# Attention with 64 heads on one core: Q and K rows interleaved by dimension, V and ones in alternate columns, seven output buffers, other planner numbers and a rewritten end

## The chip, the core and the metric

The kernel runs as one program on 1 core of a Trainium2 chip. Its time is the device time of one execution in microseconds (us); a kernel's time is the median of its runs. TensorE is called PE below, VectorE DVE, ScalarE ACT, GpSimd POOL and SyncE SP, as the profile does.

## The reference

Two attentions over the same 2048 tokens, 32 heads of 16 dimensions each, are mixed by a gate. In A all heads share one K and one V, in B every head has its own.

```
def _A_ref(x, wq, wk, wv, wo):          # H = 32, Dh = 16, S = 2048, D = 512
    q = (x @ wq).reshape(B, S, H, Dh).transpose(0, 2, 1, 3)
    k = x @ wk
    v = x @ wv
    scores = jnp.einsum("bhqd,bkd->bhqk", q, k) * (Dh ** -0.5)
    p = _softmax(scores, axis=-1)
    o = jnp.einsum("bhqk,bkd->bhqd", p, v)
    return o.transpose(0, 2, 1, 3).reshape(B, S, H * Dh) @ wo
...
x = A_x
g = _sigmoid((x * gate_w).sum(-1, keepdims=True))
a = _A_ref(x, A_wq, A_wk, A_wv, A_wo)
b = _B_ref(x, B_wqkv, B_wo)             # as A, but q, k, v all per head, from one wqkv
return g * a + (1 - g) * b
```

## The kernel before

**Work and stages.** The 64 heads go in eight groups of eight, alternately from A and B (`groups`, n = 0 to 7). A group has two halves of the queries, and a half has two parts, q = 0 and q = 2, of two head pairs each. That makes 32 phases. In a phase 32 key blocks ("quads") are worked for two head pairs, so a phase has 64 score tiles, the kernel 2048. A score tile is [128 keys, 2 heads x 512 queries]: PE multiplies K with Q into PSUM (`products`), ACT takes exp of it into an SBUF tile called prob (`score`, line 622), and PE multiplies V with that (`values`, line 663). Two PSUM buffers named sc hold the scores. A stationary operand of V has 32 columns, 16 of V and 16 of ones, so numerator and denominator of the softmax come out of one product, summed in a third PSUM buffer over the phase.

**Exp on VectorE.** Some score tiles skip ACT. Their scores go to the other PSUM buffer of the two named `pair`, and DVE computes exp in seven instructions (`chain`): a conversion to int32 (line 816), two bit operations (819, 823) and four steps of a polynomial (828). The results lie in tiles named vec.

**Precision.** Q and K are split into a high and a low fp16 half. A head's 16 dimensions take 64 rows: Q has high, low, high, low and K has high, high, low, low, 16 rows each. `lay` (line 383) moves the halves from the projection to these rows by DMA, on the queues of SP and POOL.

**The end of a phase.** `emptied` has DVE copy the sums to an SBUF tile raw (line 722). `normalised` moves the denominators to a tile dT and the numerators to oT by ten DMAs on SP (line 546); DVE then takes reciprocals (553), multiplies (556), and splits into o16, high and low (559, 562). `o_unit` multiplies o16 with the output weights on PE, DVE scales by the gate into a tile named sum (line 506), and a DMA adds it to the output. In the last group (n = 7) the sum is made in SBUF instead, in `late`, which lies in the memory of xT (line 500).

**What sets the order.** The whole program is written out by a planner that runs when the kernel is built. `_Plan` carries estimated clocks of the engines; `pe_step` chooses what PE does next (a score tile, a piece of `values`, or a step of another unit); `plan.vector` chooses what DVE does next. `vector_job` decides when a score tile goes to DVE: not while more than WORK nanoseconds of chain work are queued, not without three free vec tiles, and from within the last MOST quads of a phase, or the next phase when fewer than CHAIN nanoseconds are left. A projection of Q may begin EARLY quads ahead of the half before the one that needs it. `hurry` gives other units precedence when their due time is near, with JOB, AFTER and SPARE as their prices. Engines run what they are given in order and wait on semaphores, so a wrong estimate shows as a wait, not as another order.

**The end of the kernel.** After the last exp (lines 1225 to 1237) the last raw is normalised in four pieces of 128 tokens; ACT makes the high half (559), POOL the low half (562), PE three products per piece into the same PSUM buffer, DVE two adds (500), and SP and ACT send two blocks out.

Of the kernel before, what the change touches and what calls it, by code (L numbers as in the profile page):

```python
# [49 lines left out]
ISSUE, ISSUE_SP, LANDS, SUM_LANDS = 480, 600, 3200, 6500  # L50
PROBS, VECS = 6, 7

# [112 lines left out]
def _fast(ctx, tc, x, wq_a, wk_a, wv_a, wo_a, wqkv_b, wo_b, gate_w, out, flag):  # L165
# [165 lines left out]
    def kv_split(h, bank):  # L331
# [3 lines left out]
        k32 = ops.tile([P, 2, 4, DH], F32, tag="k32", name=f"k32{h}", bufs=1)  # L335
        kn = sums[1][:, h].bitcast(F16).rearrange("p (i a b d) -> p i a b d", i=8, a=2, b=4)
        ts = slice(8 * h, 8 * h + 8)

        def take(queue=nc.sync, key=True, value=True):
            if key:  # L340
                nc.vector.tensor_scalar(k32, pk[:, :, :, :DH], UP ** -1, None, op0=ALU.mult)
            if value:
                for d in (0, 2 * DH):
                    v = vA[0][:, ts, d : d + DH].rearrange("p (e i) d -> p e i d", e=2)
                    nc.vector.tensor_scalar(v, pk[:, :, :, DH : 2 * DH], UP ** -2, None, op0=ALU.mult)
                swapped(vA[1][:, ts], vA[0][:, ts], queue)
                nc.vector.tensor_copy(z[:, ts].rearrange("p (e i) -> p e i", e=2), pk[:, :, :, 2 * DH])
# [13 lines left out]
    def k_turn(kn, bank, i):  # L361
        pkt = bank[:, 0].bitcast(F16)
        nc.tensor.transpose(pkt[:, i * P : (i + 1) * P], kn[:, i].rearrange("p a b d -> p (a b d)"), ident16)

# [18 lines left out]
    def lay(hilo, to, p, parts, queues):  # L383

        fns = []
        for n, part in sorted(enumerate(parts * 2), key=lambda x: x[1]):
            hh = n // 4
            at = slice((2 * p + hh) * DH, (2 * p + hh + 1) * DH)
            dst = to[hh * ROWS + n % 4 * DH :][:DH].rearrange("d (a q) -> d a q", a=2)
            fns.append(lambda q=queues[len(fns) % len(queues)], dst=dst, src=hilo[part][at]: q.dma_start(dst, src))  # L390
        return fns
# [89 lines left out]
    def o_unit(n, half, t, qs, first, last):  # L481
# [55 lines left out]
    def normalised(n, half, q, raw, now):  # L537
# [4 lines left out]
        queues = (nc.sync, nc.scalar, nc.gpsimd) if ends else (nc.sync,)  # L542
        moves = [(d, DH, 2 * DH, 0), (d, 5 * DH, 2 * DH, 2 * DH), (o, 0, DH, 0), (o, 3 * DH, 2 * DH, DH), (o, 7 * DH, DH, 3 * DH)]
        moves = [(*move, e) for part in (0, 2) for e in range(2) for move in moves[part : part + 2 + part // 2]]
        for m, (part, at, n_rows, to, e) in enumerate(moves):
            queues[m % len(queues)].dma_start(part[ROWS * e + to :][:n_rows], raw[at : at + n_rows, e])  # L546
# [14 lines left out]
        def low(c):  # L561
            (nc.gpsimd if ends else nc.vector).tensor_sub(o16[:, 1, c : c + cut], o[:, c : c + cut], o16[:, 0, c : c + cut])

# [86 lines left out]
    def values(m, cols):  # L650
# [5 lines left out]
        for k in range(4):  # L656
            p, hh = q + k // 2, k % 2
            if src == "a":
                v = vA[w][:, c, hh * DH : (hh + 2) * DH]
            else:  # L660
                v = vB[w][:, c, p, hh : hh + 2, :].rearrange("p a d -> p (a d)")
# [47 lines left out]
    def emptied(t):  # L709
# [10 lines left out]
        def take():  # L720
            state["raw"] = ops.tile([P, 2, BLK], F32, tag="raw", name=f"raw{ph}", bufs=1)
            nc.vector.tensor_copy(state["raw"], full)  # L722

# [285 lines left out]
    def flag_stats():  # L1009
        absmax("v_a", 0, vA[0][:, :, :DH], AX.XY)  # L1010
        absmax("gate", 0, wkv16[0][:, 0, :, 2 * DH])
# [123 lines left out]
    pair_q = (nc.sync, nc.gpsimd)  # L1135
    moves = [lay(hilo, to[p], p, (0, 1, 0, 1), (nc.scalar,) * 2 + pair_q * 3 if p == 1 else pair_q) for p in range(4)]
    for move in moves[0][:4] + moves[1][:4] + moves[0][4:] + moves[1][4:]:
        move()
# [85 lines left out]

    over, times, high, low = tail[0]
    last = [o_unit(len(groups) - 1, 1, t, (2,), False, True) for t in range(4)]
    over(0), times(0), high(0), low(0)
    for t in range(4):
        if t < 3:
            c = (t + 1) * P  # L1230
            over(c), times(c), high(c), low(c)
        for fn, _ in last[t].jobs:
            fn()
        last[t].finish(plan.pe)
        for op in plan.ops:
            op.fn()
        plan.ops.clear()

# [148 lines left out]
```

## Time and profile before

| | before |
|---|---|
| median of 3 runs | 1860.64 us (1858.08 to 1861.57) |
| the profiled execution: own time, span | 1863.72 us, 1861.9 us |
| busy: ACT, PE, DVE, POOL | 1797.5, 1760.7, 1217.5, 392.0 us |
| exp tiles on ACT in the trace | 1932 into prob, 12 into vec |
| exp tiles on DVE (line 816) | 104 |
| granted PE clock, mean | 0.992 |

The span is from the first instruction to the last; the profiled execution's own time holds 1.8 us more around it. Busy time is the union of an engine's instructions. A row of the groups gives the count, the busy time, the mean length of one instruction in ns and then the idle time of the engine ahead of it with what ended it. A row of the timeline gives start and length in us.

### The profile page before, as it was taken

The page shows a single profiled execution, that of the slowest core. Times are in us where ns is not written, and L with a number is a line of the kernel's source. Part 1 is how long each engine was busy: PE and PEld are TensorE (multiplying, and loading weights), DVE is VectorE, ACT ScalarE, POOL GpSimd, SP SyncE. Part 2 cuts the span into 40 slices and gives each one's busy share as a digit, 9 for nine tenths or more (in the row PEclk, how much of TensorE's full clock was granted, in tenths as well). Part 3 has the DMA queues.
Part 4 walks back from the last instruction along what each step waited for, and adds up shares of the span by engine and source line. Part 5 has one row for each costly group of instructions (what it writes and reads, how often), then busy time and mean ns, then how long its engine had stood idle before and what let it go on. Part 6 is the DMA issues. An engine that isn't in the chain of part 4 may idle for free.

```text
span 1861.9 us, 97691 instructions
## 1 busy us (share of the span) xinstructions
PE 1760.7 (95%) x45403; PEld 859.8 (46%) x45403; DVE 1217.5 (65%) x1369; ACT 1797.5 (97%) x1959; POOL 392.0 (21%) x575
## 2 busy tenths in 40 slices
PE   9999999999999999999999999999999999998994
PEld 5544454444444444444444445444444444443441
DVE  4267323969686772678677684297868677349963
ACT  4999999999999999999999999999999999999993
POOL 4213103232031211412112320242202320130000
PEclk9999999999999999999999999999999999999997
DMA  5121212223142322412224240252313322234011
GB/s 146 41 60 43 82 32 55 82 57 57 32 79 40 66 49 59 83 35 54 43 50 75 51 80 21 51 97 48 57 40 54 65 53 45 51 66 124 24 49 59
DMA packets 75678, 109.69 MB, mean 59 GB/s; under 512 B 22256, under 2 KB 30672, under 8 KB 75264
## 3 DMA queue, kind: packets, MB, share of 16 engines
q0 software_dynamic: 27904, 44.24, 14.1%
q1 hardware_dynamic: 43920, 56.51, 11.9%
q8 instruction: 357, 5.85, 1.4%
q10 hardware_dynamic: 3440, 2.62, 0.4%
q14 instruction: 57, 0.47, 0.1%
HBM read 14.82 MB, written 33.55 MB: 26 GB/s over the span
## 4 chain that ended last, share of the span: by engine, by line
ACT 74%; PE 11%; issue 8%; DVE 5%; DMA 1%; SPq 1%; POOL 0%; ACTq 0%; DVEq 0%
ACT prob L622 74%; PE pair L663 5%; PE sc L608 3%; DVE vec L828 2%; PE pair L207 2%; DVE vec L816 1%; SPq L546 1%; DVE xT L500 0%; DVE dT L553 0%; DVE sum L506 0%; PE pt L294 0%; PE pair L294 0%; PE pair L457 0%; DVE vec L819 0%; DVE raw L722 0%
## 5 line engine op out<-in xcount | busy, mean ns | idle before, releaser
L622 ACT ACTIVATE prob<-sc 128x1024 f32<-128x1024 f32 x1932 | 1777.0, 1125 | 12.3 <-PE sc L608 10.4
L663 PE MATMUL pair<-prob,vA 64*32 64x512 f32 (+1 forms) x8168 | 521.8, 566 | 0.8 <-issue 0.8
L663 PE MATMUL pair<-prob,vB 64*32 64x512 f32 (+1 forms) x8112 | 521.7, 570 | 0.5 <-issue 0.5
L608 PE MATMUL sc<-Qb,K 64*32 64x512 f16 x7744 | 409.5, 381 | 47.0 <-ACT prob L622 38.7
L608 PE MATMUL sc<-Qa,kA 64*32 64x512 f16 x7808 | 409.5, 381 | 20.4 <-ACT prob L622 12.3
L608 PEld LDWEIGHTS <-K 64*32 64x32 f16 x8192 | 203.8, 90 | 422.9 <-issue 382.9
L608 PEld LDWEIGHTS <-kA 64*32 64x32 f16 x8192 | 202.9, 90 | 390.3 <-issue 349.9
L828 DVE SCALAR_TENSOR_TENSOR vec<-vec,vec 128x1024 f32<-128x1024 f32 x312 | 378.3, 1224 | 2.6
L663 PEld LDWEIGHTS pair<-prob,vA 64*32 64x32 f32 x8168 | 158.7, 105 | 23.7 <-issue 4.8
L663 PEld LDWEIGHTS pair<-prob,vB 64*32 64x32 f32 x8112 | 157.8, 105 | 22.2 <-issue 2.7
L816 DVE TENSOR_SCALAR vec<-pair 128x1024 int32<-128x1024 f32 x104 | 126.4, 1215 | 51.6 <-PE pair L608 49.3
L828 DVE SCALAR_TENSOR_TENSOR vec<-vec 128x1024 f32<-128x1024 f32 x104 | 131.3, 1263 | 1.2
L516 POOL DMA_DIRECT2D out_dram<-sum x48 | 60.1, 1253 | 340.7 <-DVE sum L506 330.8
L553 DVE RECIPROCAL dT<-dT 128x256 f32<-128x256 f32 (+1 forms) x66 | 111.4, 1693 | 28.2 <-DMA dT<-raw 28.2
L722 DVE COPY raw<-pair 128x1024 f32<-128x1024 f32 x32 | 39.2, 1224 | 115.3 <-PE pair L663 115.2
L506 DVE TENSOR_SCALAR sum<-pair,gate_up 128x512 f32<-128x512 f32 x112 | 79.2, 742 | 49.2 <-PE pair L207 49.1
L390 POOL DMA_DIRECT2D K<-hikb x64 | 31.1, 491 | 341.7 <-DVE hikb L431 340.9
L390 POOL DMA_DIRECT2D Qa<-hiqa x63 | 31.9, 511 | 335.7 <-DVE hiqa L431 316.9
L207 PE MATMUL pair<-w16ob,o 64*32 64x512 f16 x1536 | 66.1, 392 | 14.8 <-ACT o L559 6.9
L823 DVE TENSOR_SCALAR vec<-vec 128x1024 int32<-128x1024 int32 x104 | 78.1, 751 | 0.0
L819 DVE TENSOR_SCALAR vec<-vec 128x1024 int32<-128x1024 int32 x104 | 75.2, 723 | 1.4
L431 DVE TENSOR_SCALAR hivb<-pair 128x1024 f16<-128x1024 f32 x8 | 9.8, 1224 | 101.2 <-PE pair L207 101.2
(149 smaller groups left out, 1272.2 us busy)
## 6 DMA issues: line engine op xcount, KB each, us to landing
out_dram<-sum POOLq DMA_DIRECT2D x48, 512.0 KB, 6.1
dT<-raw SPq DMA_DIRECT2D x126, 64.0 KB, 3.0
vB<-vB SPq DMA_DIRECT2D x16, 384.0 KB, 3.8
out_dram<-sum SPq DMA_DIRECT2D x8, 512.0 KB, 3.8
xT<-out_dram SPq DMA_DIRECT2D x16, 256.0 KB, 5.0
oT<-raw SPq DMA_DIRECT2D x126, 32.0 KB, 2.9
oT<-raw SPq DMA_DIRECT2D x62, 64.0 KB, 2.9
vec<-in_A_x_dram SPq DMA_DIRECT2D x14, 256.0 KB, 4.9
```

The lines of the kernel that those rows point to most:

```text
L207: nc.tensor.matmul(outs[n : n + COLS, i], lhs[i][rows(i), n : n + COLS], rhs[i][rows(i)], start=start, stop=stop)
L390: fns.append(lambda q=queues[len(fns) % len(queues)], dst=dst, src=hilo[part][at]: q.dma_start(dst, src))
L506: nc.vector.tensor_scalar(state["sum"][:, e], pair[1][:, e], g, None, op0=ALU.mult)
L516: done = plan.on_pool([lambda: nc.gpsimd.dma_start(dst, state["sum"], accum_op=ALU.add)], t, 1300)
L553: nc.vector.reciprocal(d[:, c : c + cut], d[:, c : c + cut])
L608: nc.tensor.matmul(bank[a : a + COLS, hh], k[rows(hh), key : key + COLS], Q[src, gi, half, p][rows(hh), j * BLK : (j + 1) * BLK], start=Tr ...
L622: nc.scalar.activation(probs[u], sc, AF.Exp, scale=SCALE / (UP * UP))
L663: nc.tensor.matmul(pair[0][32 * k : 32 * k + 32, i, cols], v[rows(i)], probs[2 * m + k // 2][rows(i), hh, cols], start=first, stop=last)
L816: nc.vector.tensor_scalar(tile("p").bitcast(I32), pair[1], SCALE / (UP * UP) / math.log(2) * 2.0 ** 23, None, op0=ALU.mult)
L819: nc.vector.tensor_scalar(tile("m").bitcast(I32), tiles["p"].bitcast(I32), 0x7FFFFF, 125 << 23, op0=ALU.bitwise_and, op1=ALU.bitwise_or)
L823: nc.vector.tensor_scalar(tile("w").bitcast(I32), tiles["p"].bitcast(I32), 0x7F800000, 0x40000000 | LEAD, op0=ALU.bitwise_and, op1=ALU.bit ...
L828: nc.vector.scalar_tensor_tensor(p, m if i == 3 else p, VEC[i], m if i else w, op0=ALU.add, op1=ALU.mult)
```

## The change

Seven edits are made together.

1. Q and K rows are interleaved: row 4d + part of a head instead of 16 part + d. A DMA then moves two heads (32 rows, every fourth partition), and there are four for a head pair's tile where there were eight. K of A is built in the same layout, in the memory of oT and dT instead of in a sum tile.
2. V of A: its columns alternate with ones (`[DH, 2]`), where there were V, ones, V. It is written by one instruction instead of two. In groups of A the sums then have numerators in even and denominators in odd rows, and four DMAs instead of ten carry them to oT and dT.
3. o16 has seven buffers instead of three, and the units of `o_unit` are due four quads later.
4. One vec tile fewer (VECS 6), the last two input tiles lying in the two sum tiles.
5. Planner numbers: CHAIN 28000, MOST 18, EARLY 16, AFTER 2000, WORK 5000 (from 24000, 14, 12, 3000, 1500).
6. The last copy to raw is split: the first half on DVE, the second on ACT.
7. The end is written out: four PSUM buffers for the four pieces, the low half on DVE, all eight output DMAs on SP.

```
-PROBS, VECS = 6, 7
+PROBS, VECS = 6, 6
...
-    vA = [cst.tile([P, NT, 3 * DH], F32, name=f"vA{w}") for w in range(2)]
+    vA = [cst.tile([P, NT, DH, 2], F32, name=f"vA{w}") for w in range(2)]
...
-        kn = sums[1][:, h].bitcast(F16).rearrange("p (i a b d) -> p i a b d", i=8, a=2, b=4)
+        kn = ops.tile([P, BLK], F32, tag=("oT", "dT")[h], name=f"kn{h}", bufs=1)
+        kn = kn.bitcast(F16).rearrange("p (i a d b) -> p i a b d", i=8, a=2, b=4)
...
-        for n, part in sorted(enumerate(parts * 2), key=lambda x: x[1]):
-            hh = n // 4
-            at = slice((2 * p + hh) * DH, (2 * p + hh + 1) * DH)
-            dst = to[hh * ROWS + n % 4 * DH :][:DH].rearrange("d (a q) -> d a q", a=2)
...
+        for n, part in sorted(enumerate(parts), key=lambda x: x[1]):
+            dst = to[n : n + 4 * 2 * DH - 3 : 4].rearrange("d (a q) -> d a q", a=2)
+            src = hilo[part][2 * p * DH : 2 * (p + 1) * DH]
...
-        due = 32 * (4 * n + 2 * half + 4)
+        due = 32 * (4 * n + 2 * half + 8)
...
+        if src == "a":
+            moves = [(part, slice(k, P + k - 1, 2), 0, ROWS) for k, part in ((1, d), (0, o))]
...
-        o16 = ops.tile([P, 2, BLK], F16, tag="o16", name=f"o16{n}{half}{q}", bufs=3)
+        o16 = ops.tile([P, 2, BLK], F16, tag="o16", name=f"o16{n}{half}{q}", bufs=7)
...
-            (nc.gpsimd if ends else nc.vector).tensor_sub(o16[:, 1, c : c + cut], o[:, c : c + cut], o16[:, 0, c : c + cut])
+            nc.vector.tensor_sub(o16[:, 1, c : c + cut], o[:, c : c + cut], o16[:, 0, c : c + cut])
...
+            if ph == LASTS:
+                nc.vector.tensor_copy(state["raw"][:, 0], full[:, 0])
+                nc.scalar.copy(state["raw"][:, 1], full[:, 1])
...
-    CHAIN, MOST, EARLY = 24000, 14, 12
-    JOB, AFTER, TURN, SPARE, WORK, EXTRA, LATE = 900, 3000, 3000, 5000, 1500, 7000, 0
+    CHAIN, MOST, EARLY = 28000, 18, 16
+    JOB, AFTER, TURN, SPARE, WORK, EXTRA, LATE = 900, 2000, 3000, 5000, 5000, 7000, 0
...
+    into = [pair[1], pair[0]] + [ps_s.tile([P, ACT, BLK], F32, tag="sc", name=f"end{t}") for t in range(2)]
...
+    for t in range(4):
+        high[t]()
+        if t < 3:
+            over[t + 1]()
+        elif t == 3:
+            give(1, 1)
+            give(2, 0)
+        low[t]()
+        products_of(t)
+        if t < 3:
+            times[t + 1]()
+        if t == 1:
+            give(0, 0)
+        if t == 2:
+            give(0, 1)
+            give(1, 0)
+    give(2, 1)
+    give(3, 0)
+    give(3, 1)
```

The planner's numbers move instructions on every engine. Over the whole program DVE gets 116 chains where it had 104, and ACT 1932 exp tiles where it had 1944. By phase, the number of tiles on DVE is

```
before: 0 2 4 0  0 4 4 6  2 4 4 4  0 4 4 6  2 4 4 4  0 4 4 6  2 4 4 4  0 4 6 4
after:  0 2 4 2  0 6 4 6  2 4 2 4  4 6 4 4  2 4 4 4  2 4 4 6  2 4 2 4  4 4 8 4
```

Three places show it. The first is DVE at the start of phase 12 (group 3, of B): hik, lok, hiq are halves of a projection, vec the tiles of a chain, sum the gated output. Before:

```order
L553 RECIPROCAL dT_17245<-dT_17245 128x256
L434 SCALAR_TENSOR_TENSOR lokb_17468<-pair_83,hikb_17467 128x1024
L553 RECIPROCAL dT_17245<-dT_17245 128x256
L556 SCALAR_TENSOR_TENSOR oT_17244<-oT_17244,dT_17245 128x256 x2
L559 CAST o_17256<-oT_17244 128x256 x2
L562 TENSOR_TENSOR o_17256<-oT_17244,o_17256 128x256 x2
L216 TENSOR_REDUCE stats<-hikb_17467 128x1
L506 TENSOR_SCALAR sum_110<-pair_83,gate_up 128x512 x2
L431 TENSOR_SCALAR hiqb_18315<-pair_83 128x1024
L434 SCALAR_TENSOR_TENSOR loqb_18316<-pair_83,hiqb_18315 128x1024
L216 TENSOR_REDUCE stats<-hiqb_18315 128x1
L816 TENSOR_SCALAR vec_106<-pair_83 128x1024
```

The same place after, where line 823 is what 816 was, 835 what 828 was:

```order
L823 TENSOR_SCALAR vec_105<-pair_83 128x1024
L826 TENSOR_SCALAR vec_104<-vec_105 128x1024
L830 TENSOR_SCALAR vec_107<-vec_105 128x1024
L835 SCALAR_TENSOR_TENSOR vec_105<-vec_104 128x1024
L835 SCALAR_TENSOR_TENSOR vec_105<-vec_105,vec_104 128x1024 x2
L505 TENSOR_SCALAR sum_110<-pair_83,gate_up 128x512 x2
L835 SCALAR_TENSOR_TENSOR vec_105<-vec_105,vec_107 128x1024
L556 RECIPROCAL dT_17116<-dT_17116 128x256
L823 TENSOR_SCALAR vec_108<-pair_83 128x1024
L559 SCALAR_TENSOR_TENSOR oT_17115<-oT_17115,dT_17116 128x256
L826 TENSOR_SCALAR vec_103<-vec_108 128x1024
L830 TENSOR_SCALAR vec_104<-vec_108 128x1024
```

Chains now start at once, between the normalisation's steps, where two projections stood; before, the first chain came after them.

The second place is DVE at the end, from the last copy to raw on; xT is the memory of `late`. Before:

```order
L722 COPY raw_43191<-pair_82 128x1024
L553 RECIPROCAL dT_43194<-dT_43194 128x128
L556 SCALAR_TENSOR_TENSOR oT_43193<-oT_43193,dT_43194 128x128
L553 RECIPROCAL dT_43194<-dT_43194 128x128
L556 SCALAR_TENSOR_TENSOR oT_43193<-oT_43193,dT_43194 128x128
L500 SCALAR_TENSOR_TENSOR xT<-pair_82,gate_up,xT 128x512 x2
L553 RECIPROCAL dT_43194<-dT_43194 128x128
L556 SCALAR_TENSOR_TENSOR oT_43193<-oT_43193,dT_43194 128x128
L500 SCALAR_TENSOR_TENSOR xT<-pair_82,gate_up,xT 128x512 x2
L553 RECIPROCAL dT_43194<-dT_43194 128x128
L556 SCALAR_TENSOR_TENSOR oT_43193<-oT_43193,dT_43194 128x128
L500 SCALAR_TENSOR_TENSOR xT<-pair_82,gate_up,xT 128x512 x4
```

After, as far as the second add:

```order
L726 COPY raw_42698<-pair_83 128x512
L556 RECIPROCAL dT_42702<-dT_42702 128x128
L559 SCALAR_TENSOR_TENSOR oT_42701<-oT_42701,dT_42702 128x128
L556 RECIPROCAL dT_42702<-dT_42702 128x128
L565 TENSOR_TENSOR o_42713<-oT_42701,o_42713 128x128
L559 SCALAR_TENSOR_TENSOR oT_42701<-oT_42701,dT_42702 128x128
L556 RECIPROCAL dT_42702<-dT_42702 128x128
L565 TENSOR_TENSOR o_42713<-oT_42701,o_42713 128x128
L559 SCALAR_TENSOR_TENSOR oT_42701<-oT_42701,dT_42702 128x128
L1245 SCALAR_TENSOR_TENSOR xT<-pair_83,gate_up,xT 128x512
L556 RECIPROCAL dT_42702<-dT_42702 128x128
L565 TENSOR_TENSOR o_42713<-oT_42701,o_42713 128x128
```

The low half (line 565) has come to DVE, and the adds stand one piece later than the products they add.

The third place is SP's queue at the first Q tiles, which the first exps wait for. Before:

```order
L390 DMA Qa_642<-hiqa_636 16x1024 x2
L390 DMA Qa_643<-hiqa_636 16x1024
L390 DMA Qa_642<-loqa_637 16x1024 x2
L390 DMA Qa_643<-loqa_637 16x1024 x2
L390 DMA Qa_644<-hiqa_636 16x1024 x2
```

After:

```order
L389 DMA Qa_641<-hiqa_635 32x1024
L389 DMA Qa_642<-hiqa_635 32x1024
L389 DMA Qa_641<-loqa_636 32x1024
L389 DMA Qa_642<-loqa_636 32x1024
L389 DMA Qa_643<-hiqa_635 32x1024
```

Four DMAs stand ahead of the third Q tile where seven stood.

More of the change, by code (lines that the diff above doesn't have):

```diff
@@ L542, in normalised @@
         queues = (nc.sync, nc.scalar, nc.gpsimd) if ends else (nc.sync,)
[L543 to L546, printed above, removed]
+        if src == "a":
+            moves = [(part, slice(k, P + k - 1, 2), 0, ROWS) for k, part in ((1, d), (0, o))]
+        else:
+            moves = [(d, DH, 0, 2), (d, 5 * DH, 2, 2), (o, 0, 0, 1), (o, 3 * DH, 1, 2), (o, 7 * DH, 3, 1)]
+            moves = [(part, slice(at, at + n * DH), to * DH, n * DH) for part, at, to, n in moves]
+        moves = [(*move, e) for t in (d, o) for e in range(2) for move in moves if move[0] is t]
+        for m, (part, at, to, n_rows, e) in enumerate(moves):
+            queues[m % len(queues)].dma_start(part[ROWS * e + to :][:n_rows], raw[at, e])
         plan.sp = max(plan.sp, now) + len(moves) * ISSUE_SP
-        o16 = ops.tile([P, 2, BLK], F16, tag="o16", name=f"o16{n}{half}{q}", bufs=3)
+        o16 = ops.tile([P, 2, BLK], F16, tag="o16", name=f"o16{n}{half}{q}", bufs=7)
         o16s[n, half, q] = o16
@@ L658, in values @@
             if src == "a":
[L659 removed]
+                v = vA[w][:, c].rearrange("p d s -> p (d s)")
             else:
@@ L1135, in _fast @@
     pair_q = (nc.sync, nc.gpsimd)
-    moves = [lay(hilo, to[p], p, (0, 1, 0, 1), (nc.scalar,) * 2 + pair_q * 3 if p == 1 else pair_q) for p in range(4)]
-    for move in moves[0][:4] + moves[1][:4] + moves[0][4:] + moves[1][4:]:
+    moves = [lay(hilo, to[p], p, (0, 1, 0, 1), (nc.scalar,) + pair_q * 2 if p == 1 else pair_q) for p in range(4)]
+    for move in moves[0][:2] + moves[1][:2] + moves[0][2:] + moves[1][2:]:
         move()
@@ L1223, in _fast, with products_of, give @@
             plan.vector()
-    over, times, high, low = tail[0]
-    last = [o_unit(len(groups) - 1, 1, t, (2,), False, True) for t in range(4)]
-    over(0), times(0), high(0), low(0)
+    over, times, high, low = ([lambda c=c * P, step=step: step(c) for c in range(4)] for step in tail[0])
+    n = len(groups) - 1
+    src, gi = groups[n]
+    w = weights[src, gi, "o"]
+    into = [pair[1], pair[0]] + [ps_s.tile([P, ACT, BLK], F32, tag="sc", name=f"end{t}") for t in range(2)]
+    def products_of(t):
+        for k, (a, b) in enumerate(PARTS):
+            lhs = [o16s[n, 1, 2][:, a, t * P : (t + 1) * P]] * 2
+            by_tiles(into[t], lhs, [w[e ^ 1][:, b] for e in range(2)], k == 0, k == len(PARTS) - 1)
+    def give(t, e):
+        tt, mine = 8 + 4 * e + t, late[:, 4 + t, e]
+        nc.vector.scalar_tensor_tensor(mine, into[t][:, e], gate_up[:, 1, tt : tt + 1], mine, op0=ALU.mult, op1=ALU.add)
+        nc.sync.dma_start(out[tt * P : (tt + 1) * P, :], mine)
+    over[0]()
+    times[0]()
     for t in range(4):
+        high[t]()
         if t < 3:
[L1230 to L1237, printed above, removed]
+            over[t + 1]()
[14 more added lines that the diff above has]
+    give(3, 1)
 def _sigmoid(nc, gate, z, scale):
```

14 lines of the change are left out of this document (7 added, 7 removed).

## The prediction

> **What bounds the kernel now.** I read the page first: who is busy, and what the chain that ended last consists of. The fence has the page's busy line, its chain by engine, and its group of exps.
>
> ```profile
> PE 1760.7 (95%) x45403; PEld 859.8 (46%) x45403; DVE 1217.5 (65%) x1369; ACT 1797.5 (97%) x1959; POOL 392.0 (21%) x575
> ACT 74%; PE 11%; issue 8%; DVE 5%; DMA 1%; SPq 1%; POOL 0%; ACTq 0%; DVEq 0%
> L622 ACT ACTIVATE prob<-sc 128x1024 f32<-128x1024 f32 x1932 | 1777.0, 1125 | 12.3 <-PE sc L608 10.4
> ```
>
> ACT and PE both look full, but a modelled PE end says little. So I asked for the stages (window, its length, then PE, PEld, DVE, ACT, POOL busy), the waits, and ACT in order of time.
>
> ```profile
> 400.00:800.00 400.00, 386.47 (x10056) 188.09 (x10044) 275.98 (x302) 399.60 (x436) 89.27 (x124) 1.00 0.30 58
> PE sc L608 <- ACT prob L622: 51.0, 143, 0.6
> 1253.78 335.57 ACT L622 ACTIVATE prob<-sc 128x1024 f32<-128x1024 f32 x365 [0.52 <-PE sc L608]
> ```
>
> In the middle ACT has 0.4 us free in 400, and PE's score products wait for ACT 143 times. The last row gives the pace: 365 exps in 335.57 us, 0.919 us each (the mean of 1125 ns counts the overlap of neighbours twice). Is PE close behind? The next rows are PE's timeline over one pair of exps with two fillers, and one without.
>
> ```profile
> 912.49 0.41 PE L608 MATMUL sc<-Qb,K 64*32 64x512 f16 x8
> 912.71 0.63 PE L207 MATMUL pair<-xT,w16vb 64*32 64x512 f16 x16
> 913.25 0.41 PE L608 MATMUL sc<-Qb,K 64*32 64x512 f16 x8
> 913.47 1.05 PE L663 MATMUL pair<-prob,vB 64*32 64x512 f32 x16
> 914.33 0.41 PE L608 MATMUL sc<-Qb,K 64*32 64x512 f16 x8
> 926.09 0.41 PE L608 MATMUL sc<-Qb,K 64*32 64x512 f16 x8 [0.35 <-ACT prob L622]
> ```
>
> Start to start a score group takes 0.22 us and the value products 0.86. Two projection groups are 2 x 0.22 = 0.43, yet the next score stands 0.54 behind their start: 0.11 us of that waits. With no filler 0.35 us is waited openly. So ACT paces this kernel between the first exp and the last, and a microsecond taken from ACT there is a microsecond of the span, as long as PE gets its operands.
>
> **Part 1: twelve exps go from ACT to DVE.** By the order ACT has 1932 exp tiles where it had 1944, and DVE 116 chains where it had 104. On ACT that is 12 x 0.919 = 11.0 us less. DVE pays for it; the fence has the five groups of a chain.
>
> ```profile
> L828 DVE SCALAR_TENSOR_TENSOR vec<-vec,vec 128x1024 f32<-128x1024 f32 x312 | 378.3, 1224 | 2.6
> L816 DVE TENSOR_SCALAR vec<-pair 128x1024 int32<-128x1024 f32 x104 | 126.4, 1215 | 51.6 <-PE pair L608 49.3
> L828 DVE SCALAR_TENSOR_TENSOR vec<-vec 128x1024 f32<-128x1024 f32 x104 | 131.3, 1263 | 1.2
> L823 DVE TENSOR_SCALAR vec<-vec 128x1024 int32<-128x1024 int32 x104 | 78.1, 751 | 0.0
> L819 DVE TENSOR_SCALAR vec<-vec 128x1024 int32<-128x1024 int32 x104 | 75.2, 723 | 1.4
> ```
>
> Busy time by count, a chain is (378.3 + 126.4 + 131.3 + 78.1 + 75.2) / 104 = 7.6 us, so twelve are 91 us: DVE goes from 1217.5 to about 1308 of some 1845 us, 71%. That costs nothing where DVE has room, but the room is uneven. With group means, the densest stretch between two copies to raw (30, in the last group) has 49.7 us of DVE work beside 58 exps of 53.3 us before (0.93), and 50.6 us beside 56 exps of 51.5 us after (0.98). Stretches above 0.9 are six after, two before. What is behind DVE there is PE: it runs in order, and value products that find their vec tile unfinished hold up the scores behind them, so ACT starves. Counted in the order, from a chain's scores to the first use of its result, the tightest chain had 1.4 us to spare and has 1.0; four had under 2 us, seven have. In the trace the wait came once:
>
> ```profile
> PE pair L663 <- DVE vec L828: 0.3, 1, 0.3
> ACT prob L622 <- PE sc L608: 10.4, 17, 2.9
> ```
>
> Of ACT's 10.4 us of waits for scores the longest, 2.9, is ahead of the first exp. Few causes change with the edit, so I add 1 us for the dense stretches; bounds -1 (fewer waits) and +6.
>
> **Part 2: half as many moves, other layouts.** The moves of Q and K (32 rows instead of 16) and of raw in groups of A (four instead of ten) carry the same bytes with fewer issues. SP and POOL are not on the chain (1% and 0% above), PE's stationary tiles keep their 32 columns, and o16's buffers and the later due time only shift fillers, which the 0.11 to 0.35 us of PE's waits hide; gone, that cover would cost up to the 0.22 us of a group. I cost all this at nothing after the start. At the start it shows. The rows are PE's second score group, ACT's second exp, SP's queue, and DVE's two steps on K and V.
>
> ```profile
> 32.68 0.92 PE L608 MATMUL sc<-Qa,kA 64*32 64x512 f16 x8 [0.49 <-DMA Qa<-loqa]
> 33.65 4.81 ACT L622 ACTIVATE prob<-sc 128x1024 f32<-128x1024 f32 x5 [0.39 <-PE sc L608]
> 28.55 2.43 SPq L390 DMA_DIRECT2D Qa<-loqa  x4
> 28.15 0.29 DVE L355 COPY sum<-sum 128x512 f16<-128x512 f16 x1
> 28.36 0.48 DVE L345 TENSOR_SCALAR vA<-pair 128x128 f32<-128x128 f32 x2
> ```
>
> The second score waits for a move issued seventh or later; now it is fourth, about 1.2 us earlier, and the 0.39 us gap on ACT goes: -0.4. Against that, DVE's copies of K are written with a stride of four elements, ahead of PE's transposes and so of the first exp. Between no change and the speed of a same-sized f32 instruction (0.74, line 500 below) the large copy costs 0 to +0.45, the two small ones up to +0.1 each; one write of V goes, -0.24. I take +0.1, nearer the unstrided row; bounds of the whole start -0.7 and +0.4. [...]
>
> **Part 3: the end.** The rows are DVE from the last copy to raw, the first piece's low half on POOL, PE behind it and at the last piece, and the last issue; then the groups of single sizes.
>
> ```profile
> 1831.75 1.22 DVE L722 COPY raw<-pair 128x1024 f32<-128x1024 f32 x1 [10.56 <-PE pair L663]
> 1837.86 0.29 DVE L556 SCALAR_TENSOR_TENSOR oT<-oT,dT 128x128 f32<-128x128 f32 x1 [1.00 <-DMA oT<-raw]
> 1842.46 0.81 POOL L562 TENSOR_TENSOR o<-oT,o 128x128 f16<-128x128 f32 x2 [7.43 <-issue]
> 1842.93 0.63 PE L207 MATMUL pair<-w16ob,o 64*32 64x512 f16 x8 [3.34 <-POOL o L562]
> 1851.12 1.48 PE L207 MATMUL pair<-w16ob,o 64*32 64x512 f16 x24 [1.53 <-DVE xT L500]
> 1852.67 1.41 DVE L500 SCALAR_TENSOR_TENSOR xT<-pair,gate_up,xT 128x512 f32<-128x512 f32 x2 [1.60 <-PE pair L207]
> 1854.11 0.34 ACTq L502 DMA_DIRECT2D out_dram<-xT  x1
> L500 DVE SCALAR_TENSOR_TENSOR xT<-pair,gate_up,xT 128x512 f32<-128x512 f32 x24 | 16.8, 742 | 22.6 <-PE pair L207 22.6
> L553 DVE RECIPROCAL dT<-dT 128x128 f32<-128x128 f32 x4 | 3.8, 946 | 2.9 <-DMA dT<-raw 2.9
> ```
>
> Two things stretch the end: POOL begins its first low half at 1842.46, and one PSUM buffer makes every piece go products, adds, products. From the first normalised piece (1837.86) to the last add (1852.67 + 1.41 = 1854.08) are 16.2 us. With four buffers and the low half on DVE, what is left is DVE's own queue: from the first multiply, four of those (0.29), three reciprocals (0.95), four low halves (0.29 for 128 x 128, as the multiply; not seen on DVE) and eight adds (0.74): 1.2 + 2.8 + 1.2 + 5.9 = 11.1 us. Neighbours overlap (two adds take 1.41, not 1.48), up to 0.07 at each of 18 steps, so 9.9 to 11.1; I take 10.7, with PE's last products covered by an add but for 0.2. That is -5.5. PE needs 4 x 1.48 = 5.9 us within it, at the slow pace of the 24-matmul row, so it is hidden. The split copy halves the 1.22 us ahead of the moves (one half on DVE as an add's 0.74, ACT's beside it): -0.5. Together -6.0, bounds -4.5 and -7.0. Eight issues of 0.34 us on SP fit between adds.
>
> **The sum.** -11.0 + 1.0 - 0.3 - 6.0 = -16.3 us. The profiled execution took 1863.7 (span 1861.9 and 1.8 around it); after: 1847.4. The median of the runs, 1860.64, lies 3.1 below the profiled one, so I forecast 1860.6 - 16.3 = 1844.3. Bounds of the terms: -11.0 - 1 - 0.7 - 7.0 = -19.7 (1840.9) and -11.0 + 6 + 0.4 - 4.5 = -9.1 (1851.5).
>
> **Rivals.** *PE becomes the bound.* If the pace in the packed stretches were PE's own, removing exps would give nothing there, and only start and end remain: -6.3, 1854.3. For it: PE is 97% busy in the 400 us window. Against it: the waits of 0.11 and 0.35 us, which 12 fewer exps in 1944 (0.006 us per exp) do not use up. 0.15.
>
> *DVE falls behind in the six dense stretches, and it gets slower.* A hold-up of DVE that exceeds a chain's 1 to 2 us of spare goes through PE to ACT. The rows are DVE's longest stall for a raw move, and a short DVE cast stretched while POOL splits weights.
>
> ```profile
> 274.67 3.37 DVE L553 RECIPROCAL dT<-dT 128x256 f32<-128x256 f32 x2 [4.84 <-DMA dT<-raw]
> 1237.30 1.25 DVE L559 CAST o<-oT 128x256 f16<-128x256 f32 x1
> 1236.92 1.48 POOL L225 TENSOR_TENSOR w16ob<-wob,w16ob 128x512 f16<-128x512 f32 x1
> ```
>
> One stall of 4.84 us past 1.0 us of spare costs 3.8 us; in each of six stretches 23 us, so -16.3 + 23 = +6.7, 1867.3. It decides from 16.3 / 6 = 2.7 us per stretch. Against it: stretch 30 was at 0.93 before and PE waited 0.3 us for vec in the whole run; and DVE's moves get shorter queues in A. The cast ends at 1238.55, POOL's instruction at 1238.40. [...] 0.06.
>
> *The change does nothing*: the twelve tiles were in ACT's waits, and the end is set by DMA landing. 1860.6. The last add was 7.8 us before the span's end in any case, and ACT has no such waits. 0.03.
>
> **The numbers.** Forecast 0.76, rivals 0.15, 0.06, 0.03. The time is the forecast's 1844.3. The range, 1839 to 1854, takes the bounds of the terms (1840.9 to 1851.5), 2 us for the runs' own spread (1858.1 to 1861.6) and most of the first rival. A difference under 0.2% (3.7 us) can't be told from none here: faster 0.91, same 0.03, slower 0.06.
>
> **What would show it.** Right: ACT's exp group at 1920 in prob with the same 0.919 us pace, its waits near 10 us, no gap at the second exp, and from the copy to raw to the last add about 16 us instead of 22. Wrong: waits of PE for vec tiles or of ACT for scores that grow by more than 6 us, above all in the last two groups; or value products in even step with no wait for ACT.

## The result, and the profile after

| | before | after |
|---|---|---|
| median of 4 runs each | 1860.70 us (1858.08 to 1861.57) | 1845.58 us (1844.44 to 1845.86) |
| ratio, 95% interval | | 0.992 (0.9903 to 0.9937) |
| the profiled execution: own time, span | 1863.72, 1861.9 us | 1845.49, 1843.6 us |

The change made the kernel 15.1 us faster by the medians; 1844.3 was forecast. The spans differ by 18.3 us, since the profiled execution of before was 3.0 us above its median and that of after was at its own. What follows compares spans, piece by piece.

First the page of the kernel after: busy time of each engine, and the group of exps.

```profile
PE 1749.8 (95%) x45259; PEld 848.3 (46%) x45259; DVE 1292.8 (70%) x1455; ACT 1785.5 (97%) x1948; POOL 297.6 (16%) x379
L625 ACT ACTIVATE prob<-sc 128x1024 f32<-128x1024 f32 x1920 | 1764.7, 1130 | 13.1 <-PE sc L611 11.7
```

Its waits (total, times, longest).

```profile
ACT prob L625 <- PE sc L611: 11.7, 13, 2.7
PE pair L666 <- DVE vec L835: 0.9, 1, 0.9
```

One long row of ACT's timeline.

```profile
1314.02 353.95 ACT L625 ACTIVATE prob<-sc 128x1024 f32<-128x1024 f32 x385 [0.62 <-PE sc L611]
```

Twelve exps are gone from ACT, the pace is unchanged (353.95 / 385 = 0.919 us), ACT's waits for scores went from 10.4 to 11.7 us, and PE hardly waits for DVE's chains. That is the picture that was forecast. The start is not. These are POOL's first select and ACT's first exp, before:

```profile
1.23 0.29 POOL masks.py:199 TENSOR_SCALAR_AFFINE_SELECT ident<-ident 128x128 f32<-128x128 f32 x1 [0.29 <-POOL ident masks.py:197]
32.23 1.02 ACT L622 ACTIVATE prob<-sc 128x1024 f32<-128x1024 f32 x1 [2.91 <-PE sc L608]
```

and after, with PE's first transposes, which need that select's result:

```profile
10.73 0.28 POOL masks.py:199 TENSOR_SCALAR_AFFINE_SELECT ident<-ident 128x128 f32<-128x128 f32 x1 [9.79 <-issue]
11.06 5.36 PE L294 MATMUL pt<-ident,vec 128*64 128x128 f32 x64 [5.84 <-POOL ident masks.py:199]
35.83 5.61 ACT L625 ACTIVATE prob<-sc 128x1024 f32<-128x1024 f32 x6 [2.68 <-PE sc L611]
```

POOL stands for 9.79 us with no event that the profile shows, PE waits 5.84 us for it, and the first exp comes 3.6 us later. The six exps in one row show that the gap at the second exp is gone. Now the last exps, before and then after, and after's end: the two half copies to raw, the first reciprocal and multiply, the last adds, SP's issues.

```profile
1799.19 31.38 ACT L622 ACTIVATE prob<-sc 128x1024 f32<-128x1024 f32 x34
```

```profile
1797.89 23.94 ACT L625 ACTIVATE prob<-sc 128x1024 f32<-128x1024 f32 x26 [0.21 <-issue]
1823.02 0.69 DVE L726 COPY raw<-pair 128x512 f32<-128x512 f32 x1 [3.44 <-PE pair L666]
1823.74 0.59 ACT L727 COPY raw<-pair 128x512 f32<-128x512 f32 x1 [1.91 <-DVE raw L726]
1827.37 0.95 DVE L556 RECIPROCAL dT<-dT 128x128 f32<-128x128 f32 x1 [3.67 <-DMA dT<-raw]
1828.62 0.29 DVE L559 SCALAR_TENSOR_TENSOR oT<-oT,dT 128x128 f32<-128x128 f32 x1 [0.29 <-DMA oT<-raw]
1835.93 2.06 DVE L1245 SCALAR_TENSOR_TENSOR xT<-end,gate_up,xT 128x512 f32<-128x512 f32 x3
1832.01 6.34 SPq L1246 DMA_DIRECT2D out_dram<-xT  x8
```

| piece of the span, us | before | after | difference | forecast |
|---|---|---|---|---|
| to the first exp | 32.23 | 35.83 | +3.6 | +0.1 |
| first exp to the end of the last | 1798.34 | 1786.00 | -12.3 | -10.4 |
| to the last copy to raw | 1.18 | 1.19 | 0.0 | 0 |
| copy to raw to the end of the last add | 22.33 | 14.97 | -7.4 | -6.0 |
| behind the last add | 7.8 | 5.6 | -2.2 | 0 |

Each column is one execution, and that of before holds 3.0 us above its median; which piece they lie in can't be told. The sum came out near the forecast, and its first piece is 3.5 us off, against -2.0 us in the sum of all. The experiments ask where the 3.6 us at the start come from, which edit brings the twelve exps, and how far that goes.

### The profile page after: what moved, and what is told of

Read it like the earlier page. It is cut to its first block, busy times and chain, and to the rows that moved or that the text cites. A ratio compares the mean times of both kernels' runs of the same rounds, so it can differ in the third digit from the quotient of the medians.

```text
span 1843.6 us, 96794 instructions
## 1 busy us (share of the span) xinstructions
PE 1749.8 (95%) x45259; PEld 848.3 (46%) x45259; DVE 1292.8 (70%) x1455; ACT 1785.5 (97%) x1948; POOL 297.6 (16%) x379
## 5 line engine op out<-in xcount | busy, mean ns | idle before, releaser
L625 ACT ACTIVATE prob<-sc 128x1024 f32<-128x1024 f32 x1920 | 1764.7, 1130 | 13.1 <-PE sc L611 11.7
L666 PE MATMUL pair<-prob,vB 64*32 64x512 f32 (+1 forms) x7856 | 510.3, 577 | 0.4 <-issue 0.4
L611 PE MATMUL sc<-Qb,K 64*32 64x512 f16 x7632 | 399.7, 380 | 44.1 <-ACT prob L625 33.7
L835 DVE SCALAR_TENSOR_TENSOR vec<-vec,vec 128x1024 f32<-128x1024 f32 x348 | 425.2, 1233 | 3.6
L823 DVE TENSOR_SCALAR vec<-pair 128x1024 int32<-128x1024 f32 x116 | 140.9, 1215 | 55.6 <-PE pair L611 55.4
L666 PEld LDWEIGHTS pair<-prob,vB 64*32 64x32 f32 x7856 | 151.8, 105 | 19.9 <-issue 1.8
L835 DVE SCALAR_TENSOR_TENSOR vec<-vec 128x1024 f32<-128x1024 f32 x116 | 142.4, 1227 | 1.2
L826 DVE TENSOR_SCALAR vec<-vec 128x1024 int32<-128x1024 int32 x116 | 82.5, 711 | 1.6
L830 DVE TENSOR_SCALAR vec<-vec 128x1024 int32<-128x1024 int32 x116 | 82.0, 707 | 0.0
L389 POOL DMA_DIRECT2D Qb<-hiqb x32 | 17.7, 553 | 366.2 <-DVE hiqb L430 363.2
L207 PEld LDWEIGHTS <-o 64*32 64x32 f16 x3072 | 50.8, 93 | 42.5 <-ACT o L562 8.5
```

The lines of the kernel that those rows point to most:

```text
L207: nc.tensor.matmul(outs[n : n + COLS, i], lhs[i][rows(i), n : n + COLS], rhs[i][rows(i)], start=start, stop=stop)
L611: nc.tensor.matmul(bank[a : a + COLS, hh], k[rows(hh), key : key + COLS], Q[src, gi, half, p][rows(hh), j * BLK : (j + 1) * BLK], start=Tr ...
L625: nc.scalar.activation(probs[u], sc, AF.Exp, scale=SCALE / (UP * UP))
L666: nc.tensor.matmul(pair[0][32 * k : 32 * k + 32, i, cols], v[rows(i)], probs[2 * m + k // 2][rows(i), hh, cols], start=first, stop=last)
L823: nc.vector.tensor_scalar(tile("p").bitcast(I32), pair[1], SCALE / (UP * UP) / math.log(2) * 2.0 ** 23, None, op0=ALU.mult)
L826: nc.vector.tensor_scalar(tile("m").bitcast(I32), tiles["p"].bitcast(I32), 0x7FFFFF, 125 << 23, op0=ALU.bitwise_and, op1=ALU.bitwise_or)
```

## The experiments

Every ratio is to the kernel before, run beside it, and so can differ a little from a comparison of medians taken at different times. Line numbers shift by a few between kernels.

**The end alone.**

```
 before, with the end (lines 1225 to 1237) of after, and
-            (nc.gpsimd if ends else nc.vector).tensor_sub(...)
+            nc.vector.tensor_sub(...)
```

> The kernel before with edit 7 alone (four buffers, low half on DVE, eight output DMAs on SP), the last copy to raw unsplit; ACT keeps 1944 exp tiles. The prediction's own term for the end without the split is -5.5, so 1855.2 us. The two traces read together (14.97 us from the copy to raw to the last add where there were 22.33, and about 2 us less behind the last issue) say -9, so 1851.5. Rival (the end is set by when transfers land, not by the queue of adds): 1860.7, no change.

Measured 1858.57 us, ratio 0.9984 (0.9975 to 0.9993): 3 us, far less than both estimates. The rows are POOL's select, the first exp, the copy to raw and the last adds.

```profile
10.75 0.28 POOL masks.py:199 TENSOR_SCALAR_AFFINE_SELECT ident<-ident 128x128 f32<-128x128 f32 x1 [9.81 <-issue]
36.26 1.02 ACT L622 ACTIVATE prob<-sc 128x1024 f32<-128x1024 f32 x1 [2.58 <-PE sc L608]
1835.29 1.22 DVE L722 COPY raw<-pair 128x1024 f32<-128x1024 f32 x1 [10.56 <-PE pair L663]
1848.88 2.25 DVE L1238 SCALAR_TENSOR_TENSOR xT<-end,gate_up,xT 128x512 f32<-128x512 f32 x3
```

The end itself shrank, from 22.33 to 1848.88 + 2.25 - 1835.29 = 15.84 us. But the late select came with it, and the first exp is 4.0 us later. So the late start comes with the new end.

**The numbers, the layouts, and all but the numbers.**

```
 numbers_alone: before, with
+    CHAIN, MOST, EARLY = 28000, 18, 16
+    JOB, AFTER, TURN, SPARE, WORK, EXTRA, LATE = 900, 2000, 3000, 5000, 5000, 7000, 0
 layouts_alone: before, with edits 1 and 2
 old_numbers: after, with
+    CHAIN, MOST, EARLY = 24000, 14, 12
+    JOB, AFTER, TURN, SPARE, WORK, EXTRA, LATE = 900, 3000, 3000, 5000, 1500, 7000, 0
```

> The kernel before with edit 5 alone, the planner's numbers. By the order this gives DVE fewer chains, not more: 96 where there were 104, so ACT has 1952 exp tiles. Theory (ACT's pace of 0.919 us per exp sets the middle): 8 x 0.919 = +7.4, 1868.1 us. Rival (PE is the bound in the packed stretches, or the numbers pay by a smoother order): 1860.7 or less.

> The kernel before with edits 1 and 2 alone, the rows of Q and K by dimension and the columns of V alternating with ones. By the order 1942 exp tiles are on ACT (1944 before). Theory (halved moves cost nothing after the start): 2 x 0.919 = -1.8 and -0.4 to +0.6 at the start, so 1858.4 to 1859.5 us. Rival (shorter queues of moves free more than the exps): below 1856. Second rival (the strided copies ahead of the first exp cost what the trace of after shows as a later first exp, 3.6 us): about 1862.5.

> The changed kernel with edit 5 undone: the old planner numbers, all the rest as changed. By the order 104 chains on DVE and 1944 exp tiles on ACT, as before the change. Theory (each exp taken from ACT is worth its pace): 1845.6 + 12 x 0.919 = 1856.6 us. Rival (PE is the bound, and the gain came from start and end): 1845.6.

The numbers alone gave 1898.74 us, 1.0193 (1.0178 to 1.0208): 37 us slower, where 7.4 were expected. Eight more exps are the small part; ACT's waits for scores, 10.4 us in before, are the large one. The wait row:

```profile
ACT prob L622 <- PE sc L608: 37.8, 31, 7.3
```

The longest of these waits in the timeline, with PE ahead of it and behind:

```profile
1206.20 1.49 PE L207 MATMUL pair<-w16oa,o 64*32 64x512 f16 x48 [1.42 <-DVE lokb L434]
1210.99 1.02 ACT L622 ACTIVATE prob<-sc 128x1024 f32<-128x1024 f32 x1 [7.33 <-PE sc L608]
1211.86 0.40 PE L608 MATMUL sc<-Qb,K 64*32 64x512 f16 x4 [0.94 <-DMA K<-lokb]
```

K of the next group (lokb) leaves DVE only at 1206, PE does output products meanwhile, and a score behind them still waits 0.94 us for the move of K. The layouts alone gave 1860.46 us, 0.9989 (0.998 to 0.9998), which by the ratio is 2.0 us less than before, within the theory's 1858.4 to 1859.5. Their first exps, last exps and group of exps:

```profile
32.38 5.61 ACT L625 ACTIVATE prob<-sc 128x1024 f32<-128x1024 f32 x6 [3.49 <-PE sc L611]
1791.24 40.44 ACT L625 ACTIVATE prob<-sc 128x1024 f32<-128x1024 f32 x44 [0.21 <-issue]
L625 ACT ACTIVATE prob<-sc 128x1024 f32<-128x1024 f32 x1930 | 1773.7, 1130 | 17.8 <-PE sc L611 17.3
```

The select ran at 1.24 us and the first exp at 32.38, so the strided copies are not what delays the start. But the theory's terms are not what the trace shows: from the first exp to the end of the last it takes 1831.68 - 32.38 = 1799.30 us, 1.0 more than before with two exps fewer, as ACT waits 17.3 us for scores where it waited 10.4. What is saved lies behind the last add, 4.9 us for 7.8. The old numbers gave 1860.38 us, 0.9991 (0.9982 to 1.0), 13 us slower than after by the ratios (0.0071 x 1861), and 3.8 above the theory. Their group of exps:

```profile
L625 ACT ACTIVATE prob<-sc 128x1024 f32<-128x1024 f32 x1932 | 1775.8, 1129 | 17.3 <-PE sc L611 15.7
```

The twelve exps are 11.0 us of it, and waits for scores some 4 us more (15.7 us in place of 11.7). That is 15 us, as in the traces, where the stretch of the exps is 15.5 us longer; the profiled execution is the slowest of eleven. So the new numbers lower these waits with the other edits in place, and raise them without.

**Loading POOL's code early.** In POOL's program an instruction that writes no tile stands ahead of the first select, ahead of the reduction over partitions, and in the kernel before also ahead of the first low half. The built program calls it a reload of a library, of number 0 ahead of the select and the low half and of number 1 ahead of the reduction. The end of POOL's program, before and after:

```
before: L1021 ISA | L1021 ISA highest<-each | L546 DMA x3 | L562 ISA | L562 TENSOR_TENSOR x4
after:  L1028 ISA | L1028 ISA highest<-each | L549 DMA x3
```

After has lost the last of these together with the low halves. The edit puts it back where POOL is idle:

```
         nc.gpsimd.partition_all_reduce(highest, each, P, ReduceOp.max)
+        nc.gpsimd.tensor_sub(spent, each, each)
```

> The changed kernel with one more POOL instruction, a subtraction of 128 x 16 elements right after the reduction over partitions (line 1028); nothing reads its result. In the program a load of code stands ahead of POOL's first select at the start, ahead of that reduction, and, in the kernel before alone, ahead of the first low half at the end; now it stands behind the reduction again, where POOL has 110 us with nothing to do. Theory (POOL keeps the code that it ran last from one execution to the next, so that the changed kernel loads at its start what the kernel before loaded in its end): the select runs at 1.2 us and not at 10.7, the first exp at about 32.3 and not at 35.83, so 1845.6 - 3.5 = 1842.1 us. Rival (the 9.5 us at the start have another cause, as the shorter end): 1845.6.

> The kernel before with the same added POOL instruction after its reduction (line 1021). Theory: POOL's first low half at the end no longer waits 7.43 us for nothing that the profile shows; it can follow ACT's high half, which ended at 1838.49, and not begin at 1842.46, so about 4.0 us less than the kernel before: 1857.4 us against 1861.4. The start stays as it is (select at 1.2 us). Rival (POOL's wait at the end is something else, or the single PSUM buffer makes up for it): no change, 1861.4.

After with it: 1840.12 us, 0.9884 (0.9869 to 0.9899).

```profile
1.23 0.29 POOL masks.py:199 TENSOR_SCALAR_AFFINE_SELECT ident<-ident 128x128 f32<-128x128 f32 x1 [0.29 <-POOL ident masks.py:197]
32.31 5.61 ACT L625 ACTIVATE prob<-sc 128x1024 f32<-128x1024 f32 x6 [3.47 <-PE sc L611]
1709.86 1.25 POOL L1029 PARTITION_ALL_REDUCE highest<-each  x1 [25.81 <-DVE each L1028]
1718.73 0.20 POOL L1030 TENSOR_TENSOR spent<-each 128x16 f32<-128x16 f32 x1 [7.61 <-issue]
```

The stall stands behind the reduction now, as 7.61 us in which nobody waits for POOL, and the first exp is at 32.31. The span fell by 3.5 us, as expected; by the medians it is 5.5, the profiled execution (1841.83 us) being the slowest of four, and the other 2 us have no row here. Before with it: 1858.84 us, 0.9979 (0.997 to 0.9988). The first low half, the copy to raw and the last adds:

```profile
1837.71 0.42 POOL L562 TENSOR_TENSOR o<-oT,o 128x128 f16<-128x128 f32 x1 [3.39 <-ACT o L559]
1831.04 1.23 DVE L722 COPY raw<-pair 128x1024 f32<-128x1024 f32 x1 [10.56 <-PE pair L663]
1848.27 1.41 DVE L500 SCALAR_TENSOR_TENSOR xT<-pair,gate_up,xT 128x512 f32<-128x512 f32 x2 [1.60 <-PE pair L207]
```

POOL now waits for ACT, not for nothing, and copy to last add takes 18.64 us where it took 22.33: 3.7 us of the old end were this stall.

> The kernel before with edit 7 and the early load of POOL's code, nothing else: 1944 exp tiles on ACT. It completes a square of four: the old end (1861.4), the old end with the early load (1858.8), the new end (1858.6), and both. Theory (the new end had handed its load to the start): the new end's own queue is 15.84 us from the copy to raw to the last add against 18.64 with the old end and the early load, so 2.8 us below 1858.8 and 3.5 to 4 below 1858.6: 1855 to 1856 us, the first exp near 32 us. Rival (the early load does nothing for the start of this kernel): 1858.6, the first exp near 36 us.

```
 before, with the new end as in the first experiment, and the added tensor_sub
```

Measured 1853.34 us, 0.9952 (0.9938 to 0.9966). The first exp, the added subtraction, the copy to raw and the last adds:

```profile
31.78 1.02 ACT L622 ACTIVATE prob<-sc 128x1024 f32<-128x1024 f32 x1 [2.80 <-PE sc L608]
1726.72 0.20 POOL L1023 TENSOR_TENSOR spent<-each 128x16 f32<-128x16 f32 x1 [6.71 <-issue]
1830.86 1.23 DVE L722 COPY raw<-pair 128x1024 f32<-128x1024 f32 x1 [10.56 <-PE pair L663]
1844.25 2.25 DVE L1240 SCALAR_TENSOR_TENSOR xT<-end,gate_up,xT 128x512 f32<-128x512 f32 x3
```

From the copy to the last add are 15.64 us. The square is 1 and 0.9979 for the old end, 0.9984 and 0.9952 for the new one: the early load is worth 3.9 us with the old end and 6.0 with the new, and the new end 5 us once the load is out of both. By the intervals each of the three is good to some 2 or 3 us.

**The due time, and the places for o16.**

```
 due_back: after, with            due = 32 * (4 * n + 2 * half + 4)
 three_places: the same, and      o16 = ops.tile(..., bufs=3)
```

> The changed kernel with the due time of the output units set back by four quads (the due part of edit 3 undone; seven places for o16 kept). By the order DVE gets 106 chains where it has 116, and ACT 1942 exp tiles where it has 1932. Theory (each exp is worth its pace of 0.919): 1845.6 + 9.2 = 1854.8 us, and up to 4 more if its waits for scores grow as those of the run with the old numbers did. Rival (the due time only shifts fillers, as the prediction had it, and costs nothing): 1845.6.

> The changed kernel with all of edit 3 undone: three places for o16 and the old due time, with the new planner numbers and layouts. By the order 106 chains and 1942 exp tiles on ACT, as with the old due time and seven places (1859.3 us). It tells why the new numbers alone made the kernel before 37 us slower. Theory (with three places the output units are held back and come in a jam, whatever the layouts): well above 1859, up to 1859.3 + 27 = 1886 us with waits of ACT for scores near 38 us. Rival (the old layouts, with ten moves and 16 rows each, made the jam): 1859.3.

The due time alone: 1859.28 us, 0.9986 (0.9977 to 0.9995), 12 us slower than after by the ratios. Its group of exps:

```profile
L625 ACT ACTIVATE prob<-sc 128x1024 f32<-128x1024 f32 x1930 | 1775.0, 1127 | 14.3 <-PE sc L611 12.7
```

Ten exps account for 9.2 and the wait for scores for 1.0. It is no mere shift of fillers: without it ten of the twelve added chains are not there. Three places: 1857.79 us, 0.9975 (0.9965 to 0.9984), not told apart from it. So with the old due time the number of places does not matter. This kernel has the new numbers and none of the jam that they made in the kernel before (13.3 us of waits for scores where that had 37.8); what parts the two is the layouts, the vec tile and the end. The layouts, with half the moves behind K, are the likely reason, but that step by itself was not run.

**More chains still.**

```
-TO_VEC, FROM_VEC, CHAINED = 255, 150, 130
+TO_VEC, FROM_VEC, CHAINED = 150, 50, 60
```

> The changed kernel with the planner told that a chain is handed to and from DVE faster (TO_VEC, FROM_VEC, CHAINED = 150, 50, 60 for 255, 150, 130). By the order 122 chains on DVE and 1926 exp tiles on ACT, six fewer than changed. Theory (ACT paces): 1845.6 - 5.5 = 1840.1 us. Rival 1 (PE is the bound by now): 1845.6. Rival 2 (DVE falls behind, PE's value products wait for vec tiles): waits of PE for vec and of ACT for scores grow by more than 6 us, 1846 to 1855.

Measured 1850.25 us, 0.994 (0.9927 to 0.9954): with six exps fewer, some 4 us slower than after. Its waits:

```profile
ACT prob L625 <- PE sc L611: 17.1, 18, 2.9
PE pair L611 <- DVE sum L505: 6.3, 9, 1.5
PE pair L666 <- DVE raw L729: 3.5, 5, 1.8
```

Its group of exps:

```profile
L625 ACT ACTIVATE prob<-sc 128x1024 f32<-128x1024 f32 x1914 | 1764.0, 1112 | 18.0 <-PE sc L611 17.1
```

This is the second rival's mechanism: PE waits for DVE, not for a vec tile but for a PSUM buffer that DVE has not emptied. ACT pays twice: 5.4 us more waits, and 1764.0 / 1914 = 0.9216 us of busy time for each exp, 0.0025 more than in after (4.8 us in all). The mean length of one, 1112 ns for 1130, points to fewer exps that overlap their neighbours, as they can't with a gap between them.

**Combined versions.**

```
 combined: after, with the early load, and
-            nc.vector.tensor_copy(kn[:, :, 1], kn[:, :, 0])
+            nc.vector.tensor_copy(kn[:, :, 1].rearrange("p i b d -> p i d b"), kn[:, :, 0].rearrange("p i b d -> p i d b"))
-                nc.scalar.copy(state["raw"][:, 1], full[:, 1])
+                nc.scalar.copy(vec_tiles[0][:, 1], full[:, 1])
+                state["raw"] = [state["raw"][:, 0], vec_tiles[0][:, 1]]
 combined_118: combined, with TO_VEC, FROM_VEC, CHAINED = 200, 100, 100
```

> The changed kernel with the early load of POOL's code, and two small edits: the largest copy of K at the start (line 355) reads and writes runs of 64 elements in place of single ones with a step of four, and ACT writes its half of the last raw into a tile of its own, so that it need not follow DVE's half. From the row of the unstrided copy (0.29 us) and that of the changed one (0.74) the first exp comes 0.45 us earlier; the second half of raw is ready 0.6 to 0.7 us earlier. Theory: 1840.1 - 0.45 - 0.6 = 1839.1 us, with ACT's half beginning within 0.2 us of DVE's. Rival (the two halves of one PSUM buffer can't be read at once, and the transposes of K wait for other things): 1840.1.

> As the combined kernel, with TO_VEC, FROM_VEC, CHAINED = 200, 100, 100, which by the order gives 118 chains and 1930 exp tiles on ACT, two fewer. Theory (ACT paces, and the loss with 122 chains came from waits on a handoff set too short): 1839.1 - 1.8 = 1837.3 us. Rival (the same loss begins here): 1 to 5 us slower than the combined kernel, with PE's waits for sum or raw above 3 us.

Combined: 1839.84 us, 0.9877 (0.9862 to 0.9892), not to be told from the early load alone. The largest copy of K, in after and then here, and ACT's half of raw here:

```profile
31.95 0.74 DVE L355 COPY kn<-kn 128x512 f16<-128x512 f16 x1
```

```profile
26.28 0.29 DVE L355 COPY kn<-kn 128x512 f16<-128x512 f16 x1
1818.16 0.59 ACT L727 COPY vec<-pair 128x512 f32<-128x512 f32 x1 [1.91 <-DVE raw L726]
```

The copy is fast again, but from the split of Q's first tile (hiqa) to the first exp that gives 0.2 us and not 0.45 (7.49 us, where the early load alone has 7.68). The first exp itself is at 29.82 and not at 32.31, but 2.3 of these 2.5 us lie ahead of hiqa (22.33 for 24.63), where neither edit acts. Before with the early load has hiqa at 22.69 too, so the start differs by that much between executions. ACT's half waits 1.91 us for DVE's half as before, though it is written elsewhere: the shared tile was not the reason. What orders them was not tried further.

With 118 chains: 1835.68 us, 0.9848 (0.9835 to 0.9862), faster than both kernels and than everything else here. Its first exps, last exps and group of exps:

```profile
29.64 5.61 ACT L625 ACTIVATE prob<-sc 128x1024 f32<-128x1024 f32 x6 [2.59 <-PE sc L611]
1783.41 30.39 ACT L625 ACTIVATE prob<-sc 128x1024 f32<-128x1024 f32 x33
L625 ACT ACTIVATE prob<-sc 128x1024 f32<-128x1024 f32 x1918 | 1762.9, 1128 | 11.9 <-PE sc L611 11.6
```

From the first exp to the end of the last it takes 1784.2 us, 2.3 less than combined, for two exps (1.8). By the medians it is 4.2, and the rest has no row: the profiled execution, 1838.41 us, is the slowest of five. Waits for scores stay at 11.6 us. With these settings the loss begins between 118 and 122 chains.

## Why the prediction was right, and where it was not

**What bounds it.** ACT's pace held: 0.919 us before and after, and from the first exp to the last, kernels with 1944, 1932 and 1930 exps take 1798.3, 1786.0 and 1784.2 us (before, after and combined_118).

**Part 1.** -11.0 and +1.0 were forecast; the waits for scores grew by 1.3, and the piece shrank by 12.3 - 0.4 (the gap at the second exp, which was part 2's) = 11.9, where 10.0 was forecast. Most of the 1.9 is a lower busy time of each exp, 0.9198 us (1777.0 / 1932) in before and 0.9191 (1764.7 / 1920) in after, 1.3 us in all. That the waits grew as forecast shows little: with the same exps as before they are 9.9 to 11.9 us in the kernels with another end or the early load. The size was right and the reason half right. The prediction counted chains for all edits together, but put edit 3's due time at nothing ("only shift fillers"). That step failed: without the later due time there are 106 chains, with the numbers alone 96, fewer than before, and without the numbers 104. So the 116 need the due time and the numbers together; whether they need the layouts too was not run. The total did not suffer, since the chains were counted in the finished order of all edits.

**Part 2.** At the start the layouts alone gave what was forecast: first exp +0.15, gap -0.39, together -0.24 for -0.3. That is closer than one execution of each can show: with the old layouts and the early select the first exp comes at 30.82 to 32.98 us. Behind the start "at nothing" did not hold for the layouts alone: the waits for scores rose by 6.9 us, and the stretch of the exps is 2.8 us longer than two exps fewer would make it. In after these waits are 11.7 us, so the forecast for all edits was not hurt by it. That the time of the layouts alone met its theory is luck, as the shorter tail behind the last add made up for it. The large copy came at its upper bound, +0.45 (0.74 for 0.29), the small ones at +0.08 and +0.17, and the cast and the subtraction ahead of them, which the prediction did not count as strided, at +0.08 and +0.16. Little of it shows: from hiqa to the first exp after takes 7.72 us where before took 7.57. In runs of 64 elements the same copy takes 0.29 us again (combined), where it takes 0.74 with a step of four (after); the prediction's +0.1 was nearer the unstrided row.

**Part 3.** -6.0 forecast, -7.4 measured to the last add. The queue of DVE took 9.37 us from the first multiply where 10.7 was taken (the low half 0.24 us and not 0.29; neighbours overlapped by 0.08 to 0.09 us at nearly every step). The split gave -0.5 as forecast (6.11 to 5.60 from copy to first multiply; 5.97 to 6.56 in the other kernels without it, 5.39 to 5.82 in those with it), but not as halves side by side: ACT follows DVE (1823.74 and 1823.02 us), and what helps is that the first half's moves start sooner, 0.71 us after the start of the copy and not 1.25. The step that failed is the price of moving the low half from POOL to DVE. It was costed by DVE's queue alone. The row 7.43 `<-issue` ahead of POOL's first low half was read as POOL being late; by the runs it is a stall that moves with POOL's last arithmetic, and the old end paid 3.7 us for it. Without the low half 9.79 us stand ahead of the first select, and cost the start 3.5 us. That the total was still right is luck: the middle (1.9), the queue (1.4) and the tail behind the last add (2.2, from 7.8 to 5.6 us, which no term had) brought 5.5 us more than forecast. Why the tail is shorter stays open; the layouts alone, with the old end, have 4.9 us there.

**Rivals.** PE as the bound fell: two exps fewer than in combined still made it faster. DVE falling behind did not happen in after (0.9 us of waits for vec), and did at 122 chains, through PSUM buffers that it emptied late (6.3 and 3.5 us of PE's waits). That the end was set by landing fell with the square (with the early load 1858.84 us with the old end, 1853.34 with the new).

## What to carry to other kernels

An idle stretch before an instruction that the profile gives to no releaser is a cost that can move (here 7.43 us ahead of the first low half, and 9.79 ahead of the first select once the low halves were gone): ask what it is before taking that instruction away, and look at the start of the program when the end is changed. A count of moved work for a whole change says nothing about which edit moved it; planner settings act together with the other edits, and the five of these alone made the kernel 37 us slower. Moving work to a second engine paid here by about the first one's pace (0.919 us a tile) up to 118 chains; with 122 that engine's other duty, emptying PSUM, came late (9.8 us of PE's waits in two rows), and the kernel was some 4 us slower than with 116.

## What was not expected of the hardware

Ahead of the first select, of the first low half or of the added subtraction POOL stands 6.7 to 9.8 us, with nothing in the profile but "issue" in nearly all of these rows (7.43 us in before, 9.79 in after, 7.61 in after with the early load). In 14 profiled kernels the first select ran at 1.2 us in the eight whose last POOL arithmetic was a subtraction, and at 10.3 to 10.8 in the six where it was the reduction over partitions. That fits the theory that what POOL ran last carries over from one execution of the program to the next: no run here contradicts it, and moving the last arithmetic moved the stall in each pair that was tried. A load of code has no row here, so that the stall is one was not shown directly; the stall is 6.7 to 7.6 us ahead of the first arithmetic behind the reduction, and 9.4 to 9.8 at the start.
